# Half of a spatial chunk's transposing loads, asked ahead of the chunk before it

## The chip, the cores and the metric

The kernel runs on one core of a Trainium2 chip. The metric is the device time of one execution in microseconds, as the median of several runs. TensorE does the matmuls (PE in the profile), VectorE is DVE, ScalarE is ACT, GpSimd is POOL, and SyncE (SP) issues nearly all DMAs.

## The reference

Two branches read the same x (2048 rows of 1024) and are mixed by a gate per row. Branch A is a sliding, dilated attention with 32 heads; branch B is a gated MLP whose second half is mixed along the rows by a 2048 x 2048 matrix:

```python
g = sigmoid((x * gate_w).sum(-1, keepdims=True))
a = attention(x @ wqkv, window=8, dilation=2) @ wo
z = gelu(x @ w_in)                       # 2048 x 3584
z1, z2 = z[..., :1792], layernorm(z[..., 1792:])
mixed = w_sp @ z2 + b_sp[:, None]        # along the rows
b = (z1 * mixed) @ w_out
out = g * a + (1 - g) * b
```

## The kernel before

The program is one long stream on TensorE, and the work of the other engines is laid beside it by hand. A small planner, `beat`, keeps a virtual time: each group of matmuls calls `beat.run(columns)`, which moves the time on, and work registered by `beat.at(t, fn)` is put into the program at the first such point at or behind t. So `beat` fixes the order in which instructions stand in each engine's queue; it doesn't fix times on the chip. Each queue is worked off in order. A DMA on the SP queue that waits for something holds all DMAs behind it.

The order of the stages on TensorE: the columns of z2, then q, k and v of the attention (whose softmax runs on VectorE until late), then column tiles of z1, then the spatial product, then the output.

The part that matters here:

- Line 972: `for f in range(4, NF)` makes z1's column tiles f = 4 to 13, 32 matmuls each (line 983). The weights of four tiles at a time lie in one of two w1 buffers, `w1_slots[(f // 4) % 2]`: f = 8 to 11 use the first, f = 12 and 13 the second. A finished tile is stored to `z1_d` in DRAM (line 989). At f = 12, `load_z1c(0)` (line 515) is called, which brings 1.5 MB of z1 back for chunk 0.
- Lines 996 to 1023: `g_chunk(c)` is the spatial product for the output rows 512c to 512c + 511. Each of its 14 column tiles f is a chain of 16 matmuls (line 1010) of z2 against `wsp_slots[c]`. It is called for c = 0 and 1 (lines 1449 and 1450). The rows of chunks 2 and 3 are done by `seven_products` (line 1096), with fewer multiplications on sums and differences of blocks; its matmuls are those of line 1084.
- `wsp_slots[c]` holds 512 rows of w_sp, turned, so that the summed index lies on the partitions: 16 blocks i by 4 row groups aa by 128. `load_wsp(c, aa)` (line 512) fills one row group by a transposing DMA of 128 x 2048 values (512 KB). Chunk 1's buffer is the memory of the two w1 buffers: blocks i = 0 to 7 are the first, i = 8 to 15 the second.
- Lines 1426 to 1434 register, from t0 (the end of the z1 tiles) on: chunk 3's turned loads, the same rows of chunk 2 in natural order on ScalarE's queue (`natural`, line 1028), chunk 1's turned loads at t0 + 22, 26, 30 and 34, sums of absolute values on ScalarE (`sp_sums`) and a common scaling factor out of these, and chunk 2's loads at t0 + 50.
- `load_qk` (lines 413 to 415) and `load_v` (line 417) bring the next head group's q, k and v for VectorE, `store_o` (line 420) stores a pair of groups' result.
- The tile framework gives the DMAs eight completion counters in turn, and a DMA waits until the one before it on its counter has landed.

Of the kernel before, what the change touches and what calls it, by code (L numbers as in the profile page):

```python
# [58 lines left out]
def kernel(  # L59
# [24 lines left out]
    def reg(off, n):  # L84
        return arena[:, off:off + n]
# [11 lines left out]
    def warm_up(widths):  # L97
        pw = psum.tile([P, 512], F32, name="pw", tag="ps")
        for n in widths:
# [90 lines left out]
    wsp_slots = [reg(CD_OFF, 8192).rearrange("p (i a t) -> p i a t", i=16, a=4),  # L190
                 reg(EF_OFF, 8192).rearrange("p (i a t) -> p i a t", i=16, a=4),
                 reg(CD_OFF, 8192).rearrange("p (i a t) -> p i a t", i=16, a=4),
                 reg(X_OFF, 8192).rearrange("p (i a t) -> p i a t", i=16, a=4)]
# [42 lines left out]
    wsp_v = B_w_sp.rearrange("(a t) s -> a t s", t=P)  # L236
    wo_v = A_wo.rearrange("(g h d) n -> g h d n", g=NG, h=HG, d=DH)
    sync = nc.sync
# [40 lines left out]
    beat = Beat()  # L279
# [228 lines left out]
    def load_w1(ch):  # L508
        ncol = min(512, FH - 512 * ch)
        sync.dma_start(w1_slots[ch % 2][:, :, 0:ncol], win_v[:, :, 512 * ch:512 * ch + ncol])  # L510

    def load_wsp(c, aa):
        sync.dma_start_transpose(wsp_slots[c][:, :, aa, :], wsp_v[4 * c + aa])  # L513

    def load_z1c(c):
        sync.dma_start(z1c_slots[c][:, 0:12, :].rearrange("p f t -> p (f t)"), z1_d[c, :, 0:12 * 512])

# [445 lines left out]
    def seed(v):  # L963
        ps = psum.tile([P, 512], F32, name="ps", tag="ps")
        nc.scalar.copy(ps[:], v)
        seeded.append(ps)
# [5 lines left out]
    for f in range(4, NF):  # L972
        ch = f // 4
        w1 = w1_slots[ch % 2]
        if f == 8:
            load_w1(3)
        z1s = z1s_slots[(0, 1, 2, 3, 0, 1, 3, 2, 0, 3, 1, 2, 0, 1)[f]]
        for c in range(4):
            if 4 * f + c >= 4 * NF - AHEAD:
                seed(bsp_bc[:, 0:512])  # L980
            ps = psum.tile([P, 512], F32, name="ps", tag="ps")
            for kt in range(KT):
                nc.tensor.matmul(ps[:], w1[:, kt, (f % 4) * P:(f % 4 + 1) * P], xT[:, kt, 512 * c:512 * (c + 1)],  # L983
                                 start=(kt == 0), stop=(kt == KT - 1))
            keep = f > 11 and c < 2
            nc.scalar.activation(z1c_slots[c][:, f, :] if keep else z1s[:, c, :], ps[:], ACT.Gelu_apprx_tanh)
            beat.run(KT * 512)
        c0 = 2 if f > 11 else 0
        beat.at(beat.now + (3.0 if f < 11 else 0.0), lambda f=f, c0=c0, z1s=z1s: sync.dma_start(
            z1_d[c0:4, :, f * 512:(f + 1) * 512].rearrange("c p t -> p c t"), z1s[:, c0:4, :]))  # L990
        if f == 12:
            load_z1c(0)
# [35 lines left out]
    def natural(r):  # L1028
        nc.scalar.dma_start(nat_slots[r], wsp_v[8 + r])

    def sp_sums(r):
        for k in range(2):
            src = nat_slots[r][:, 1024 * k:1024 * (k + 1)] if r < 4 else wsp_slots[3][:, 8 * k:8 * k + 8, r - 4, :]
            dst = abs_wide if r < 4 else abs_wide.rearrange("p (i t) -> p i t", t=P)
            nc.scalar.activation(dst, src, ACT.Abs, accum_out=l1[:, r, k:k + 1])
# [8 lines left out]
    def scale_sp(c, aa):  # L1044
        v = wsp_slots[c][:, :, aa, :]
        nc.scalar.activation(v, v, ACT.Copy, scale=s_up[:].bitcast(F32))
# [377 lines left out]
    t0 = beat.now  # L1424
    s_steps = whole_power(s_up, omg[:, 8:16])
    for r in range(4):
        beat.at(t0 + 2.5 * r, lambda r=r: natural(r))
        beat.at(t0 + 0.5 + 2.5 * r, lambda r=r: load_wsp(3, r))
        beat.at(t0 + 22.0 + 4.0 * r, lambda r=r: load_wsp(1, r))
        beat.at(t0 + 12.0 + 3.2 * r, lambda r=r: sp_sums(r))  # L1430
        beat.at(t0 + 25.0 + 3.2 * r, lambda r=r: sp_sums(4 + r))
        beat.at(t0 + 50.0 + 3.0 * r, lambda r=r: load_wsp(2, r))
        beat.at(t0 + 53.0 + 3.5 * r, lambda r=r: scale_sp(3, r))
        beat.at(t0 + 66.0 + 3.0 * r, lambda r=r: scale_sp(2, r))
    beat.at(t0 + 39.0, lambda: load_z1c(1))
    beat.at(t0 + 38.0, sp_power)
    for k in range(2):
# [63 lines left out]
```

## Time and profile before

| | us |
|---|---|
| timed runs, median of 3 | 677.36 (677.0 to 677.49) |
| the profiled execution, its own time | 678.08 |
| span from its first to its last instruction | 676.0 |
| TensorE busy | 668.0 (99%) |
| VectorE busy | 564.1 (83%) |
| ScalarE busy | 443.7 (66%) |
| first matmul of chunk 0 of the spatial product | 355.97 |
| first matmul of chunk 1 | 405.48 |
| first matmul of the seven products | 453.83 |

The granted clock was 0.999. Times in the profile are from the span's start. "SPq" is a DMA issue on the SP queue, and its duration is the time for which the issue holds the queue. "Landing" is the time from the issue until the data is there. The matmuls follow each other by 0.216 us, though one of them is shown with 0.379 us, since they are pipelined. In the table by stretches the DMA share counts the packets' time, overlapping packets included, so that it can exceed 1.

### The profile page before, as it was taken

Reading aid. Unit: us, or ns where it says so; the run is one execution under the profiler, and the core shown is the slowest. Engines: PE = TensorE matmul, PEld = TensorE weight load, DVE = VectorE, ACT = ScalarE, POOL = GpSimd, SP = SyncE. Lnnn points to the kernel's source line nnn. Section 1 sums busy time; section 2 is a strip of 40 time slices with the busy share of each in tenths; the row PEclk is TensorE's granted clock in tenths of the full one; section 3 lists DMA queues with packets and bytes.
Section 4 is the critical chain, followed back from the end, with each engine's and each line's share of the span. In section 5 each row is a group of like instructions: output and inputs, shape, how many; then the busy total and the mean of one; then the engine's idle time right before and its main releaser. Section 6 shows DMA issues by size and latency. Waiting matters only on the chain.

```text
span 676.0 us, 8980 instructions
## 1 busy us (share of the span) xinstructions
PE 668.0 (99%) x3244; PEld 353.7 (52%) x3295; DVE 564.1 (83%) x690; ACT 443.7 (66%) x815; POOL 35.3 (5%) x68
## 2 busy tenths in 40 slices
PE   9999999999999999999999999999999999999997
PEld 4499666666654455644444444444444444444443
DVE  4669779999998999999999789989669888766653
ACT  4369888866888599986864996827977543323322
POOL 1000010000000001140110001000001001000000
PEclk9999999999999999999999999999999999999999
DMA  8994978355495893289849998202651514222210
GB/s 237 182 174 123 227 174 236 85 128 157 101 222 173 241 326 141 81 239 273 297 174 212 184 216 207 90 1 62 213 159 34 161 37 84 70 68 66 63 47 32
DMA packets 185305, 101.34 MB, mean 150 GB/s; under 512 B 143534, under 2 KB 172588, under 8 KB 185004
## 3 DMA queue, kind: packets, MB, share of 16 engines
q1 hardware_dynamic: 184396, 98.66, 56.2%
q10 hardware_dynamic: 576, 2.10, 1.5%
q8 instruction: 26, 0.43, 0.3%
q14 instruction: 19, 0.16, 0.1%
q0 software_dynamic: 288, 0.01, 0.0%
HBM read 56.95 MB, written 29.16 MB: 127 GB/s over the span
## 4 chain that ended last, share of the span: by engine, by line
PE 92%; SPq 6%; DMA 1%; issue 1%; another core or an unknown queue 0%; ACT 0%; DVE 0%
PE ps L673 16%; PE ps L310 14%; PE ps L1084 12%; PE ps L1216 12%; PE ps L983 10%; PE ps L696 7%; PE ps L1010 7%; PE ps L1305 6%; SPq L513 6%; PE ps L758 4%; PE ps L1295 1%; DMA arena<-in_B_w_sp_dram 1%; PE pw L100 0%; PE pt L326 0%
## 5 line engine op out<-in xcount | busy, mean ns | idle before, releaser
L673 PE MATMUL ps<-arena 128*128 128x512 bf16 (+1 forms) x637 | 114.9, 336 | 0.2
L310 PE MATMUL ps<-arena 128*128 128x512 bf16 (+1 forms) x501 | 98.0, 353 | 0.6
L1010 PE MATMUL ps<-arena 128*128 128x512 bf16 x439 | 96.5, 379 | 1.5 <-DMA arena<-in_B_w_sp_dram 1.0
L673 PEld LDWEIGHTS <-arena 128*128 128x128 bf16 x640 | 83.4, 144 | 27.7
L1216 PE MATMUL ps<-arena 128*128 128x512 f16 (+1 forms) x382 | 91.3, 379 | 0.4
L1084 PE MATMUL ps<-arena 128*128 128x512 f16 (+1 forms) x385 | 84.5, 379 | 0.4
L310 PEld LDWEIGHTS <-arena 128*128 128x128 bf16 x512 | 50.3, 98 | 47.4 <-issue 0.9
L1010 PEld LDWEIGHTS <-arena 128*128 128x128 bf16 x448 | 43.8, 98 | 54.1 <-issue 1.5
L404 DVE TENSOR_TENSOR arena<-arena,att_A 128x4096 bf16<-128x4096 bf16 (+1 forms) x23 | 71.6, 3120 | 0.0
L361 DVE TENSOR_TENSOR arena<-arena 128x8192 bf16<-128x8192 bf16 (+1 forms) x20 | 71.2, 3568 | 0.3
L983 PE MATMUL ps<-arena 128*128 128x512 bf16 x314 | 68.9, 379 | 0.3
L1084 PEld LDWEIGHTS <-arena 128*128 128x128 bf16 (+1 forms) x392 | 38.4, 98 | 46.3 <-issue 0.2
L1216 PEld LDWEIGHTS <-arena 128*128 128x128 f16 (+1 forms) x392 | 38.3, 98 | 46.3
L364 DVE TENSOR_TENSOR arena<-arena 128x4096 bf16<-128x4096 bf16 (+1 forms) x32 | 56.2, 1756 | 0.7
L696 PE MATMUL ps<-arena 128*128 128x512 f16 (+1 forms) x224 | 52.4, 379 | 0.0
L983 PEld LDWEIGHTS <-arena 128*128 128x128 bf16 x320 | 31.3, 98 | 37.5
L1305 PE MATMUL ps<-arena 128*128 128x512 f16 (+2 forms) x199 | 50.1, 375 | 0.2
L315 ACT ACTIVATE arena<-ps 128x512 bf16<-128x512 f32 x64 | 34.1, 539 | 22.8 <-PE ps L310 22.8
L1285 DVE SCALAR_TENSOR_TENSOR arena<-ps,g_s,arena 128x512 bf16<-128x512 f32 (+1 forms) x33 | 24.0, 734 | 29.2 <-ACT arena L1337 19.9
L682 ACT CAST arena<-ps 128x512 bf16<-128x512 f32 (+1 forms) x64 | 33.2, 550 | 12.7 <-PE ps L673 12.3
L696 PEld LDWEIGHTS <-arena 128*128 128x128 f16 (+1 forms) x224 | 32.3, 144 | 16.4 <-issue 0.3
L410 DVE TENSOR_TENSOR arena<-arena 128x4096 bf16<-128x4096 bf16 x16 | 36.6, 2287 | 0.2
(213 smaller groups left out, 865.0 us busy)
## 6 DMA issues: line engine op xcount, KB each, us to landing
arena<-v_d SPq DMA_DIRECT2D x8, 960.0 KB, 6.5
arena<-k_d SPq DMA_DIRECT2D x7, 960.0 KB, 6.0
arena<-in_A_wqkv_dram SPq DMA_DIRECT2D x24, 256.0 KB, 5.0
z_d<-arena SPq DMA_DIRECT2D x12, 512.0 KB, 4.3
arena<-in_B_w_in_dram SPq DMA_DIRECT2D x5, 1024.0 KB, 6.6
o_d<-arena SPq DMA_DIRECT2D x4, 1024.0 KB, 9.5
arena<-z_d SPq DMA_DIRECT2D x15, 256.0 KB, 3.4
out_dram<-arena SPq DMA_DIRECT2D x15, 256.0 KB, 2.2
```

Source lines behind the costliest of these rows:

```text
L310: nc.tensor.matmul(ps[:, 0:N], xT[:, kt, i * P:(i + 1) * P], w2[c][:, kt, 0:N], start=(kt == 0), stop=(kt == KT - 1))
L361: TT(prod.rearrange("p (w j c) -> p w j c", w=W, j=8, c=C)[:, w0:w1], in0, in1, ALU.mult)
L364: return lambda: TT(pv[:, :, 0:half], pv[:, :, 0:half], pv[:, :, half:2 * half], ALU.add)
L404: TT(prod.rearrange("p (w j d h) -> p w j d h", w=W, j=8, d=DH, h=HG)[:, w0:w1], in0, in1, ALU.mult)
L513: sync.dma_start_transpose(wsp_slots[c][:, :, aa, :], wsp_v[4 * c + aa])
L673: nc.tensor.matmul(ps[:, n0:n1].rearrange("p (t c) -> p t c", c=C), lhsT, wgt[:, pos0:pos1, kt, :], start=(kt == 0), stop=(kt == KT - 1))
L696: nc.tensor.matmul(dst[:].rearrange("p (t c) -> p t c", c=C), lhs(k), rhs[:, :, k, :], start=first and k == 0, stop=k == 3, skip_group_che ...
L983: nc.tensor.matmul(ps[:], w1[:, kt, (f % 4) * P:(f % 4 + 1) * P], xT[:, kt, 512 * c:512 * (c + 1)], start=(kt == 0), stop=(kt == KT - 1))
L1010: nc.tensor.matmul(ps[:], z2[:, f, i, :], wsp[:, i, :, :].rearrange("p a t -> p (a t)"), start=False, stop=(i == 15), skip_group_check=True)
L1084: nc.tensor.matmul(dst[:], lhs[:, k, :], rhs(k), start=False, stop=k == 7, skip_group_check=True)
L1216: nc.tensor.matmul(dst[:], lhs[:, j, :], rhs(j), start=first and j == 0, stop=j == 6, skip_group_check=not first)
L1305: nc.tensor.matmul(dst, lhs[:, k, :], rhs[:, k, :], start=first and k == 0, stop=k == 3, skip_group_check=not first)
```

## The change

Chunk 1's four turned loads are split by the blocks i, so that each becomes two loads of 128 x 1024 values (256 KB). The first halves (h = 0) fill the memory of the first w1 buffer. They are registered at the beginning of f = 12, at 5.0, 7.2, 9.4 and 11.6 us of the planner's time from there. The second halves (h = 1) stay where the whole loads were.

```diff
+    def load_wsp_half(c, aa, h):
+        sync.dma_start_transpose(wsp_slots[c][:, 8 * h:8 * h + 8, aa, :], wsp_v[4 * c + aa][:, 1024 * h:1024 * h + 1024])
...
     for f in range(4, NF):
...
+        if f == 12:
+            for aa in range(4):
+                beat.at(beat.now + 5.0 + 2.2 * aa, lambda aa=aa: load_wsp_half(1, aa, 0))
...
-        beat.at(t0 + 22.0 + 4.0 * r, lambda r=r: load_wsp(1, r))
+        beat.at(t0 + 22.0 + 4.0 * r, lambda r=r: load_wsp_half(1, r, 1))
```

In the built order the first early half stands on SP between the z1 store of f = 11 and `load_z1c(0)`. The other three stand between the z1 store of f = 12 and `load_qk` of the last head group, ahead of the store of f = 13 and of chunk 3's turned loads. The instructions of the other engines keep their order; some of their waits name other counters.

## The prediction

> **What bounds the kernel now.** I read the page first, then the chain of waits, then the timeline of TensorE and of the SP queue around line 513, and last the busy time by stretches. The page:
>
> ```profile
> PE 668.0 (99%) x3244; PEld 353.7 (52%) x3295; DVE 564.1 (83%) x690; ACT 443.7 (66%) x815; POOL 35.3 (5%) x68
> ...
> PE 92%; SPq 6%; DMA 1%; issue 1%; another core or an unknown queue 0%; ACT 0%; DVE 0%
> ```
>
> TensorE is busy for 668.0 of the span's 676.0 us. A change that touches no matmul can win only what is left, and most of that lies before the first matmul and after the last. The chain gives 6% to the SP queue; that is where to look.
>
> The chain of waits in order of time (start us, us, what), its part before chunk 1, and then TensorE's timeline from 330 to 460 us:
>
> ```profile
> 385.67 9.53 SPq L513
> 395.30 2.20 SPq L513
> 397.54 2.50 SPq L513
> 400.10 5.25 DMA arena<-in_B_w_sp_dram
> 405.48 9.01 PE ps L1010 x41
> ```
>
> ```profile
> 355.97 48.51 PE L1010 MATMUL ps<-arena 128*128 128x512 bf16 x219
> 405.48 48.51 PE L1010 MATMUL ps<-arena 128*128 128x512 bf16 x220 [1.00 <-DMA arena<-in_B_w_sp_dram]
> 453.83 6.42 PE L1084 MATMUL ps<-arena 128*128 128x512 bf16 x28
> ```
>
> Chunk 0 of the spatial product starts at 355.97, chunk 1 at 405.48, the products after it at 453.83. Chunk 1 therefore takes 453.83 - 405.48 = 48.35 us without a stall. Chunk 0 is as long, so TensorE was ready for chunk 1 at 355.97 + 48.35 = 404.32. It waited 405.48 - 404.32 = **1.16 us** for the last of chunk 1's four turned loads, issued at 400.10 and landed at 405.35. (The row says 1.00, because the modelled end of a matmul overlaps the next by 0.16.) No other wait of TensorE after the start comes near it: the groups of matmuls have 0.0 to 0.6 us of idle time each, the group of line 1010 has 1.5.
>
> Why the last load is late is in the SP queue's timeline, and in the busy time by stretches (PE, PEld, DVE, ACT, POOL busy, clock, DMA share, GB/s):
>
> ```profile
> 349.88 0.36 SPq L989 DMA_DIRECT2D z_d<-arena  x1
> 354.99 0.33 SPq L414 DMA_DIRECT2D arena<-q_d  x1
> 355.37 0.43 SPq L415 DMA_DIRECT2D arena<-k_d  x1
> 356.79 0.37 SPq L989 DMA_DIRECT2D z_d<-arena  x1
> 357.26 27.00 SPq L513 DMA_TRANSPOSE arena<-in_B_w_sp_dram  x4
> 384.36 0.52 SPq L418 DMA_DIRECT2D arena<-v_d  x1
> 384.98 0.63 SPq L422 DMA_DIRECT2D o_d<-arena  x1
> 385.67 17.63 SPq L513 DMA_TRANSPOSE arena<-in_B_w_sp_dram  x4
> ```
>
> ```profile
> 344.00:350.00 6.00, 5.95 (x29) 2.72 (x28) 5.90 (x4) 3.02 (x6) 0.00 (x0) 1.00 0.62 206
> 350.00:357.00 7.00, 7.00 (x34) 3.16 (x33) 6.86 (x6) 4.44 (x9) 0.38 (x4) 1.00 0.57 186
> 357.00:372.00 15.00, 14.89 (x69) 6.82 (x70) 13.48 (x13) 5.57 (x11) 0.00 (x0) 1.00 1.12 228
> 372.00:385.00 13.00, 12.95 (x61) 5.88 (x61) 8.73 (x12) 12.91 (x27) 0.00 (x0) 1.00 1.13 164
> 385.00:405.00 20.00, 19.37 (x89) 8.62 (x88) 16.71 (x22) 19.81 (x42) 0.02 (x1) 1.00 1.12 230
> ```
>
> From 357 to 405 the DMA engines are full (share 1.12 to 1.13). SP is held by the four loads for chunk 3 (27.00 us), then v and o, then chunk 1's four (17.63 us). From 344 to 357 the share is only about 0.6 and SP stands idle for most of the time.
>
> **The change, part by part.** *The early halves.* Four loads of 256 KB are put ahead. In the built order the first stands behind the z1 store of f = 11 (issued 343.63) and ahead of load_z1c(0) (346.74); the other three stand behind the store of f = 12 (349.88 + 0.36 = 350.24) and ahead of load_qk (354.99), the store of f = 13 and chunk 3's loads. Their target was the w1 buffer of f = 8 to 11, and f = 12 and 13 follow with 2 x 32 matmuls of 0.216 us, 13.8 us before 355.97: it is free at 342.1, so the halves wait for no matmul.
>
> The duration: 256 KB turned loads are in the trace at other places. Line 484 has a median of 1.28 us on SP (least 1.23, most 3.28), line 547 1.31; the 512 KB loads of line 513 have a least of 2.20 and a median of 3.49. Two halves cost 2.56 against 2.20, so the split costs about 0.36 us of SP per load, 1.4 us in all, none of it TensorE's. The Trainium skill ("DMA: Bandwidth & Descriptors", section "Rules for kernel authors") speaks against such a split: it asks for large transfers and for small ones to be put together. The trace agrees in direction (205 GB/s at 1.28 us, 238 at 2.20), and if half of the loss fell on the late halves they would land 0.7 us later, which the sum below has room for.
>
> The first half has SP free for 2.5 us (it waited at 516 for a store to land), so it costs nothing. The other three are bounded from both sides. On a quiet queue they take 3 x 1.28 = 3.84, end at 354.1, before load_qk's own time, and delay nothing. Under load, at half of the loaded rows (5.11 and 10.94), they take 7.7 to 16.4 us and end at 357.9 to 366.7. I take a value between, by the data ahead of them: load_z1c(0) needs 6.7 us from its issue (median of that size), so it is in at 353.4, and 3 x 1.28 behind it ends at 357.2. Then load_qk is issued 2.2 us late. It has cover: its q and k are first read by the product at 383.40 on VectorE. Behind it the f = 13 store goes at 358.1 and chunk 3's first load at about 358.6 in place of 357.26, **1.3 us late**. Chunk 3's loads feed sums on ScalarE from 387.75 to 400.5, and ScalarE ran these without waiting.
>
> The loads share eight completion counters in turn, and four more move them by four places: the ScalarE queue's natural rows now wait for early halves to land. The second (issued 360.05) waits for the last early half: 357.2 less 1.28 plus a landing of 4.2 (line 547) is 360.1, no wait to speak of. Behind it on ScalarE are chunk 0's copies and seeds, and these are five tiles (5 x 3.46 = 17 us) ahead of TensorE.
>
> *The late halves.* From v's issue (384.36) to the last landing (405.35) are 20.99 us, in which about 4 MB move (1 of v, 1 of o, 2 of chunk 1). One MB less at that rate is 5.2 us less. Bounds: half of the three undisturbed issues, (2.20 + 2.50 + 3.20) / 2 = 4.0; half of all four (17.43 / 2) = 8.7. I take 5.2, since the DMA engines are full there. The last half lands at 405.35 + 1.3 - 5.2 = **401.4**, 2.9 us before TensorE is ready at 404.32. The stall of 1.16 us goes.
>
> A row and a rule on the 1.3 us: the loads at 362.41 and 370.83 took 8.38 and 10.94 us while the natural rows moved on ScalarE's queue, the next one 2.44. The Trainium skill ("DMA: Bandwidth & Descriptors", section "Queues, rings and completion order") says that an engine with work on several queues takes a packet of each in turn. The trace agrees: 256-byte packets of the turned loads against 4096-byte ones. By that rule a later start of chunk 3's loads is partly absorbed, as they wait for the natural rows anyway: the last half would land between 400.1 and 401.4, and the slide told of below would be less likely than its rows alone make it.
>
> *What is late next.* TensorE begins chunk 1 1.16 us earlier, and the rest must keep up. VectorE is dense from 402 to 449, but waits for TensorE's results at 449.6 to 451.2 (1.59) and before 452.30 (0.69), so it moves up by more than 1.16. The nearest later one is the sums for the second of the seven products: they end at 467.92, and are needed by its third product at 453.83 + 12.10 + 3.46 = 469.39, 1.47 us of room. Chunk 2's loads wait for chunk 0's last matmul, at 404.5 in both, and z1c(1), behind the late halves, moves up. I find nothing that takes the 1.16 us back.
>
> **Sum.** Span 676.0 - 1.16 = 674.8; the profiled execution 678.08 - 1.16 = 676.92. The median of the timed runs is 677.36, 0.72 below the profiled one; the change comes off it as it stands: **676.20**, which is -0.17%. About 0.2% (1.35 us) is what a measurement of this kernel can tell from no change, so the likeliest outcome is just inside "same".
>
> **Rivals.** *The timed runs stall by another length.* The wait hangs on DMA times, and the runs spread from 677.0 to 677.49. If the 0.72 us of the profiled run are stall, the timed gain is 0.44: 676.9. If the timed runs wait longer by as much as their spread (0.49), it is 1.65: 675.7, faster by 0.24%. For the first speaks that the profiled run is the slowest; for the second, nothing but the spread.
>
> *The gain is taken back behind chunk 1.* If VectorE does not follow, the sums at 467.92 leave 0.3 us at best; a VectorE half a microsecond behind that returns 0.2: 676.4.
>
> *Slower: the three early halves hold SP, and all behind it slides.* Place: SP from 350.24. If they do not end before the natural rows start (359.63), they crawl as chunk 3's loads did, at 5.5 us each. At the worst they end at 366.7, 11.7 us behind load_qk's time; with the smaller saving of 4.0 the last late half lands at 405.35 + 11.7 - 4.0 = 413.1, a stall of 8.7, 7.6 more than now: 684.9. With the saving of 5.2 it decides from a slide of 4.2 us on (2.9 + 1.3), where a stall is back; from 5.4 on it is slower than before and from 6.7 on measurably. Against it: load_z1c(0) is the only large transfer then, and DMA share is 0.57.
>
> *The change does not do what it says.* Excluded by the built order: the eight half loads stand where described, and chunk 1's first matmul waits for four loads, its ninth for the other four.
>
> **Chances.** Stall gone, within 0.2%: 0.48. Stall gone and more than 1.35 us in the timed runs: 0.30 (only 0.19 us more than the profiled stall is needed). Partly returned or smaller: 0.06, also within. The slide: 0.16, nearly all of it slower. The range goes from the long stall, 675.7, to no gain at all, 677.4; the slide beyond it is left out, with a little below.
>
> **What would show it.** Chunk 1 follows chunk 0 by 48.35 us, with no wait for in_B_w_sp; the chain has no SP queue at 360 to 400; SP shows half loads near 344 and 350 to 357, load_qk at 355 to 357.2, chunk 3's first load near 358.6, and four late halves that end before 400. DMA share at 344 to 357 rises towards 1. I am wrong if SP's early halves last beyond 359.6, if chunk 1 still waits, or if another wait of about 1 us shows behind 453.

## The result, and the profile after

The change made the kernel slower, by a little under 1%. Six runs of the changed kernel have a median of 683.93 us (680.55 to 687.38), six of the kernel before on the same chip 677.53 (677.0 to 677.7). The ratio is 1.0095, with a 95% interval of 1.0078 to 1.0112. The profiled execution took 687.38 us, its span 685.5, which is 9.5 us more than the profiled 676.0 of before. It is the slowest of its six, so the profile shows the loss large.

The page of the changed kernel, its busy line, its chain, and the row of the spatial product (line 1010 before, 1016 now):

```profile
PE 670.5 (98%) x3244; PEld 353.9 (52%) x3295; DVE 563.9 (82%) x690; ACT 444.0 (65%) x815; POOL 35.3 (5%) x68
...
PE 29%; DVE 2%; issue 0%; ACT 0%; DVEq 0%
...
L1016 PE MATMUL ps<-arena 128*128 128x512 bf16 x439 | 98.4, 383 | 5.3 <-ACT ps L968 4.6
```

The wait for `in_B_w_sp` is gone from the row. In its place TensorE waits 4.6 us for line 968. That is a seed: ScalarE copies the starting values of a tile into PSUM, and TensorE adds on top. The chain, followed back from the last instruction, breaks off on VectorE at about 462 us and no longer leads to SP: the engine that was late, ScalarE, is one that the prediction had taken for covered. TensorE's timeline from 357 to 560 us (start, us, what, and in brackets the idle time before it and its releaser):

```profile
357.30 34.87 PE L1016 MATMUL ps<-arena 128*128 128x512 bf16 x157
394.94 1.56 PE L1016 MATMUL ps<-arena 128*128 128x512 bf16 x5 [2.77 <-ACT ps L968]
396.72 17.33 PE L1016 MATMUL ps<-arena 128*128 128x512 bf16 x73 [0.22 <-issue]
415.90 45.05 PE L1016 MATMUL ps<-arena 128*128 128x512 bf16 x204 [1.84 <-ACT ps L968]
460.79 3.62 PE L1090 MATMUL ps<-arena 128*128 128x512 bf16 x16
465.98 12.26 PE L1090 MATMUL ps<-arena 128*128 128x512 f16 x55 [1.57 <-DVE arena L1067]
479.17 69.33 PE L1090 MATMUL ps<-arena 128*128 128x512 f16 x314 [0.93 <-DVE arena L1078]
548.34 10.74 PE L1222 MATMUL ps<-arena 128*128 128x512 bf16 x48
```

The 9.5 us are made up as follows. Chunk 0 begins 1.33 us later (357.30 against 355.97). This comes from the start of the kernel, long before the changed lines: at 36.50 us against 35.15 TensorE is that far behind already, mostly by 1.0 us in which line 310 waited for loads of w_in. Chunks 0 and 1 take 460.79 - 357.30 = 103.49 us, where two chunks without a stall take 2 x 48.35 = 96.70. So they lose 6.79, and lost 1.16 before: +5.63. The seven products take 548.34 - 460.79 = 87.55 against 84.70 before: +2.85. What follows them is 0.31 shorter. 1.33 + 5.63 + 2.85 - 0.31 = 9.5.

Why the seeds were late is in ScalarE's timeline, in the groups of the natural rows (line 1029 before, 1035 now), and on SP. First ScalarE from 366 to 388 us:

```profile
366.51 0.59 ACT L968 CAST ps<-arena 128x512 f32<-128x512 bf16 x1 [1.51 <-DMA arena<-k_d]
...
371.17 0.59 ACT L968 CAST ps<-arena 128x512 f32<-128x512 bf16 x1 [2.72 <-DMA z_d<-arena]
371.69 0.58 ACT L1024 CAST arena<-ps 128x512 bf16<-128x512 f32 x1
385.08 1.06 ACT L1041 ACTIVATE arena<-arena 128x1024 bf16<-128x1024 bf16 x1 [12.81 <-DMA arena<-in_B_w_sp_dram]
...
387.93 0.58 ACT L968 CAST ps<-arena 128x512 f32<-128x512 bf16 x1
```

ScalarE works its queue in order. At 372.27 it came to the sum over the first natural row and stood there for 12.81 us, with chunk 0's next seeds behind it in its queue. The landing times of the four natural rows, of the kernel before and then of the changed one:

```profile
L1029 ACTq DMA_DIRECT2D arena<-in_B_w_sp_dram x4: 335/366/448, 359.6 to 366.5; - x4
...
DMA to landing us min/median/max: 8.4/14.4/17.0
```

```profile
L1035 ACTq DMA_DIRECT2D arena<-in_B_w_sp_dram x4: 334/357/699, 361.0 to 370.8; - x4
...
DMA to landing us min/median/max: 20.1/23.5/25.1
```

The first two were issued 1.3 us later, as the whole stage was. The third and fourth came 3.1 and 4.3 us later (366.13 and 370.79): before these issues ScalarE waited 1.51 us for k and 2.72 for a store of z1 to land. ScalarE uses neither, so these are waits for completion counters. But all four needed 20 to 25 us instead of 8 to 17, the first one too. The SP queue at the same time:

```profile
351.63 5.43 SPq L516 DMA_TRANSPOSE arena<-in_B_w_sp_dram  x3
357.11 0.58 SPq L414 DMA_DIRECT2D arena<-q_d  x1
...
358.74 35.95 SPq L513 DMA_TRANSPOSE arena<-in_B_w_sp_dram  x4
394.79 0.53 SPq L418 DMA_DIRECT2D arena<-v_d  x1
395.41 0.63 SPq L422 DMA_DIRECT2D o_d<-arena  x1
396.10 11.63 SPq L516 DMA_TRANSPOSE arena<-in_B_w_sp_dram  x4
```

The early halves stand and end where the prediction put them (how far this is luck is said below). But chunk 3's four loads (line 513) took 35.95 us instead of 27.00. So two streams became slower together, for the same bytes: the turned loads on SP and the natural rows on ScalarE's queue. The busy time by stretches (PE, PEld, DVE, ACT, POOL busy, clock, DMA share, GB/s) shows it best, the two streams' time before and then after:

```profile
359.60:384.30 24.70, 24.59 (x114) 11.19 (x115) 19.22 (x23) 17.52 (x35) 0.00 (x0) 1.00 1.13 184
```

```profile
361.00:394.80 33.80, 31.05 (x142) 13.96 (x143) 15.89 (x16) 13.63 (x26) 0.00 (x0) 1.00 1.14 149
```

The DMA engines are as busy as before (1.14 against 1.13) and move 149 GB/s instead of 184. They are not short of work; they do it more slowly. In what follows this state is called the crawl. The packets themselves show it, counted from the trace by their size. In the changed kernel from 366 to 390 us a 256-byte packet of the turned loads took 18 ns in the median, but 115 in the mean: 39% of them took over 150 ns, and these make up 90% of the time. For the 4096-byte packets of the natural rows the mean is 315 ns. In the run below that lets the two streams move one behind the other ("held until the natural rows are in") the means are 20 and 166 ns. The kernel before stands between them (65 and 253 ns from 366 to 382 us), so it has a milder form of the same slowness.

### The profile page after: what moved, and what is told of

It reads as the page before. It is cut to its first block, busy times and chain, and to the rows that moved or that the text cites. A ratio compares the mean times of both kernels' runs of the same rounds, so it can differ in the third digit from the quotient of the medians.

```text
span 685.5 us, 8986 instructions
## 1 busy us (share of the span) xinstructions
PE 670.5 (98%) x3244; PEld 353.9 (52%) x3295; DVE 563.9 (82%) x690; ACT 444.0 (65%) x815; POOL 35.3 (5%) x68
## 5 line engine op out<-in xcount | busy, mean ns | idle before, releaser
L1016 PE MATMUL ps<-arena 128*128 128x512 bf16 x439 | 98.4, 383 | 5.3 <-ACT ps L968 4.6
L989 PE MATMUL ps<-arena 128*128 128x512 bf16 x314 | 68.9, 379 | 0.3
L315 ACT ACTIVATE arena<-ps 128x512 bf16<-128x512 f32 x64 | 34.1, 539 | 24.1 <-PE ps L310 24.1
```

Source lines behind the costliest of these rows:

```text
L1016: nc.tensor.matmul(ps[:], z2[:, f, i, :], wsp[:, i, :, :].rearrange("p a t -> p (a t)"), start=False, stop=(i == 15), skip_group_check=True)
```

## The experiments

Theories at the outset: the natural rows wait behind other completion counters, since four more DMAs shift them; more bytes ahead of load_qk and chunk 3's loads; something in the turned loads themselves; or the two streams disturbing each other when they start in a certain order. Each ratio is to the kernel before on the same chip, whose medians were 677.48 to 677.65.

**One, two and three of the early halves.** The edit, with n = 1, 2 or 3; the other row groups stay whole and late:

```diff
-            for aa in range(4):
+            for aa in range(n):
...
-        beat.at(t0 + 22.0 + 4.0 * r, lambda r=r: load_wsp_half(1, r, 1))
+        beat.at(t0 + 22.0 + 4.0 * r, lambda r=r: load_wsp_half(1, r, 1) if r < n else load_wsp(1, r))
```

> Only the first row group's half load goes early (ahead of load_z1c(0)); row group 0's other half and the other three whole loads stay in the late place. Contention (the early loads ahead of load_qk push q, k and the f = 13 store into the natural rows and chunk 3's turned loads, which then crawl together): nothing new is ahead of load_qk, so the natural rows land as before (8 to 17 us after their issue), ScalarE does not wait for them, the last turned load of chunk 1 lands about 1.3 us earlier and the stall of 1.16 us goes: 676.2 to 676.6. Counters (more DMAs move the completion counters, so that the natural rows on ScalarE's queue wait for other loads): one place moved, part of the loss is there, 678 to 681.

> Two of the four half loads go early (one ahead of load_z1c(0), one ahead of load_qk). Mixing (the natural rows on ScalarE's queue and the 256-byte packets of turned loads on SP's crawl together, and the loss depends on how much of chunk 3's first load gets through before the natural rows begin): the second half fits into SP's idle time before load_qk's own time, so chunk 3's first load starts as before: natural rows land within 17 us, 676.3 to 677.3. If every turned load ahead of load_qk costs by itself: about a third of the change's loss, 678 to 680.

> Three of the four half loads go early, two of them ahead of load_qk. Mixing: load_qk is issued up to half a microsecond late, its data are in shortly before the natural rows begin: near the edge, 676.5 to 680, with more spread than with two. If every turned load ahead of load_qk costs by itself: two thirds of the loss, 680 to 682.

Measured: 677.59 us, 1.000 [0.9991, 1.001] for one; 677.32, 1.000 [0.9991, 1.001] for two; 676.86, 0.9993 [0.9984, 1.0002] for three. The natural rows' median landing was 14.4, 10.3 and 15.7 us, load_qk went at 354.69, 355.12 and 354.99, and the wait for chunk 1's loads was gone from all three profiles. So splitting is harmless and moving is harmless, but the gain expected of the first of them (676.2 to 676.6) isn't there either. The loss comes with the fourth half, and with it load_qk is pushed for the first time, to 357.11.

**Four tiny loads, and four plain loads, added to the kernel before at the places of the early halves.** The first brings only the four DMAs (8 KB each), the second the four times 256 KB without turning:

```diff
+        if f == 12:
+            for aa in range(4):
+                beat.at(beat.now + 5.0 + 2.2 * aa, lambda aa=aa: sync.dma_start(
+                    reg(EF_OFF + 1024 * aa, 32), wsp_v[4 + aa][:, 0:32]))      # plain4: 1024 in place of 32
```

> The kernel before with four loads of 8 KB (128 x 32 values) at the places of the four early halves, into memory that the whole late loads overwrite. The counters move by four as in the change, but no bytes to speak of move. Contention: 677.4, natural rows land within 17 us. Counters: the loss of the change is there, 681 to 685, and ScalarE waits for natural rows for over 5 us.

> The kernel before with four plain (not turned) loads of 256 KB at the places of the four early halves, into memory that the whole late loads overwrite, so nothing is saved later. Contention by bytes: load_qk's data come later by about the time of these bytes, natural rows land over 18 us after their issue, TensorE stalls: 680 to 686. If only turned loads do the harm: 677.4 to 678. Counters: 681 to 685.

Measured: 677.25 us, 1.0003 [0.9992, 1.0013] for the tiny loads, natural rows 13.8 us; 677.00, 0.9991 [0.9982, 1.0001] for the plain ones, natural rows 11.4 us. Neither crawls. The shifted counters are not the cause by themselves, nor are the bytes. In the changed kernel the counters did hold two rows back, as shown above; but the first row, which no counter held, was late all the same, and the kernel with the hold on k, further down, has the wait for the store of z1 too (2.7 us) and no loss.

**The same bytes, plain, in pieces of 256 bytes.** The turned loads move 256-byte packets. Here plain loads do:

```diff
+                beat.at(beat.now + 5.0 + 2.2 * aa, lambda aa=aa: sync.dma_start(
+                    wsp_slots[1][:, 0:8, aa, :], wsp_v[4 + aa][:, 0:1024].rearrange("t (i q) -> t i q", q=P)))
```

> As the run with four plain early loads, but each written in pieces of 256 bytes (128 values for each block i), so that the early loads have the packet size of the turned ones without turning; the whole late loads overwrite them. If it is small packets ahead of load_qk that push its data back: load_qk is late by 0.5 us or more, natural rows land after 18 us, 680 to 685. If it is the turning: 677.0 to 677.6, as with large packets.

Measured: 679.23 us, 1.0031 [1.0011, 1.005], with ten runs from 676.95 to 687.49. So the early loads need not be turned for a loss; small packets at these places bring one, in part of the runs. That it is the same loss isn't shown: the profiled run (678.90) has natural rows of 16.2 us and a wait of 1.7 us for chunk 1's loads; its large losses were not profiled.

**The natural rows on SP's queue.** The changed kernel, with one word changed, so that the natural rows and chunk 3's loads alternate on one queue; later the same word in the kernel before:

```diff
-        nc.scalar.dma_start(nat_slots[r], wsp_v[8 + r])
+        nc.sync.dma_start(nat_slots[r], wsp_v[8 + r])
```

> The changed kernel with the four natural rows of chunk 2 issued on the SP queue in place of ScalarE's, at the same planner times, so that they and the turned loads go through one queue one after the other. Contention between the two queues: the crawl goes, natural rows land within 10 us of their issue, ScalarE waits for them for less than 3 us, no stall at chunk 1: 676.0 to 676.8. Contention by bytes alone, whatever the queue: 680 to 685. Counters: 680 to 685.

> The kernel before (whole loads, no early halves), with the natural rows issued on SP's queue. Mixing: natural rows land within 10 us, chunk 3's loads end at about 380, chunk 1's whole loads land by 400, the stall of before goes without any early half: 676.3 to 676.9, as the changed kernel with the same edit. If the early halves are needed for the gain: 677.3 to 677.6.

Measured, with the change: 676.73 us (676.11 to 676.86), 0.9984 [0.9975, 0.9994]. This is faster than both kernels, by 0.76 us against the kernel before. Without the change: 677.34, 0.9996 [0.9988, 1.0005], though 676.3 to 676.9 was expected and its profile shows no stall. The busy time by stretches and TensorE's timeline of the first:

```profile
357.70:379.70 22.00, 22.00 (x104) 9.94 (x103) 17.89 (x17) 12.45 (x24) 0.00 (x0) 1.00 1.10 257
```

```profile
356.38 96.86 PE L1016 MATMUL ps<-arena 128*128 128x512 bf16 x448
453.07 84.86 PE L1090 MATMUL ps<-arena 128*128 128x512 bf16 x392
```

The same rows now move at 257 GB/s, the natural rows land after 4.5 us (median), and TensorE runs both chunks and the seven products in one piece each. The early halves are all there, and load_qk goes at 356.15. The loss needs the two queues at once.

**Chunk 3's loads held until the natural rows are in.** The changed kernel, with an 8 KB store of the last natural row into a new DRAM tile n_d on SP ahead of chunk 3's loads. SP has to wait for that row:

```diff
-        beat.at(t0 + 0.5 + 2.5 * r, lambda r=r: load_wsp(3, r))
+        beat.at(t0 + 10.0 + 0.5 * r, lambda r=r: load_wsp(3, r))
...
+    beat.at(t0 + 9.0, lambda: sync.dma_start(n_d[:], nat_slots[3][:, 0:32]))
```

> The changed kernel with a store of 8 KB of the last natural row, to memory that nothing reads, on SP ahead of chunk 3's four turned loads, so that SP holds these back until the natural rows have landed. Mixing: the two never run together; natural rows land within 9 us of their issue, chunk 3's loads then take about 2.5 us each and end at 385 at the latest although they start 12 us later, ScalarE does not wait for natural rows, no stall at chunk 1: 676.0 to 677.0. If bytes or the early halves do the harm: chunk 3's loads start later and all is worse than in the change, 686 to 692.

Measured: 676.86 us, 0.9993 [0.9984, 1.0002], natural rows 6.1 us. Its SP queue:

```profile
370.22 0.32 SPq L1442 DMA_DIRECT2D n_d<-arena  x1
370.63 9.53 SPq L514 DMA_TRANSPOSE arena<-in_B_w_sp_dram  x4
380.26 0.53 SPq L419 DMA_DIRECT2D arena<-v_d  x1
```

Chunk 3's loads start 12 us later than in the changed kernel (370.63 against 358.74) and end 14.5 us earlier. Alone they take 9.53 us, not 35.95.

**Chunk 3's loads late, in the kernel before.** Is it that these loads start late against the natural rows? An 8 KB store of k ahead of them holds them until k has landed:

```diff
+    beat.at(t0 + 0.2, lambda: sync.dma_start(n_d[:], k_t[:, 14 * C:14 * C + 32]))
```

> The kernel before, with no early loads at all, and a store of 8 KB of k (just loaded) on SP ahead of chunk 3's four turned loads, to memory that nothing reads: SP holds these until k has landed, at about 362 in place of 357.3, behind the start of the natural rows (359.6). Mixing: as in the change, chunk 3's first two loads take over 25 us together (13.5 before), natural rows land 18 us or more after their issue, ScalarE waits for one of them for over 5 us; 681 to 688. If it needs the early turned halves: natural rows land within 17 us and ScalarE does not wait; everything behind is only some 4 us later, so that chunk 1 waits about 5 us: 681 to 682.

Measured: 677.58 us, 0.9998 [0.9987, 1.001]. The loads start at 363.08, 5.8 us later than before, take 20.45 us, and the natural rows land after 9.6. Both expectations had a loss; there is none, so being late does no harm by itself, and this form of the theory fell. Counted from the trace's packets, 804 KB of the natural rows had started before the first packet of chunk 3's loads, at 365.02.

**The fourth early half behind load_qk.** In the changed kernel, so that load_qk isn't pushed:

```diff
-                beat.at(beat.now + 5.0 + 2.2 * aa, lambda aa=aa: load_wsp_half(1, aa, 0))
+                beat.at(beat.now + (5.0, 7.2, 9.4, 14.1)[aa], lambda aa=aa: load_wsp_half(1, aa, 0))
```

> The changed kernel with the fourth early half moved behind load_qk and the store of f = 13, directly ahead of chunk 3's turned loads; the bytes ahead of these stay, but load_qk is no longer pushed. If the push of q and k decides: as with three early halves, 676.6 to 677.0, natural rows land within 17 us. If what decides is when chunk 3's first load gets through ahead of the natural rows: it is as late as in the change, natural rows land after 18 us, 680 to 687.

Measured: 680.26 us, 1.0038 [1.0016, 1.0059], ten runs from 676.54 to 682.95: four below 677.7, six above 679.5. The profile is of the fastest run and shows no crawl (natural rows 11.4 us). The push of load_qk isn't needed for a loss. The loss is there or not there from run to run.

**The changed kernel again, with the same hold on k, and with the natural sums later.** Three together on one chip. The hold is the edit of the kernel before, above. The other lets the four sums over natural rows stand 12 us further back among ScalarE's work, behind more seeds:

```diff
-        beat.at(t0 + 12.0 + 3.2 * r, lambda r=r: sp_sums(r))
+        beat.at(t0 + 24.0 + 3.2 * r, lambda r=r: sp_sums(r))
```

> The changed kernel once more, on the chip and beside the runs of the next two. If the loss is the crawl of the two queues, it comes in varying amounts: 678 to 688 over the runs, median about 683; natural rows landing over 18 us after their issue in the profile if that run is over 681.

> The changed kernel with the store of 8 KB of k on SP ahead of chunk 3's loads, which holds these until k has landed (about 365). Simultaneous start (the two streams crawl when both begin with all of their bytes ahead of them, and one that has a lead of half a megabyte or more gets through): the natural rows get the lead, land within 14 us, chunk 3's loads end by 386, no wait of ScalarE: 676.4 to 677.6 although these loads start 6 us later. Lateness (any later start of chunk 3's loads costs): worse than the change, 685 to 690.

> The changed kernel with the four sums over natural rows on ScalarE registered 12 us later, behind more of chunk 0's copies and seeds. The DMA side is as in the change. If ScalarE's wait for natural rows is what carries the delay to TensorE: the natural rows still land after over 18 us in slow runs, but ScalarE waits under 5 us and chunk 0 has no stall; what is left is the late chunk 3 loads and late halves, a stall of 2 to 4 us at chunk 1: median 679 to 681. If the delay comes over SP's queue alone: 682 to 685 as in the change.

Measured: the changed kernel 682.03 us, 1.0074 [1.005, 1.0097], and its second profile (685.13) crawls again: natural rows 22.1 us, chunk 3's loads 33.95, ScalarE's longest wait for a natural row 11.5; with the hold 676.60, 0.9989 [0.998, 0.9999]; with later sums 678.70, 1.0012 [0.9995, 1.0029]. SP of the second:

```profile
365.39 0.32 SPq L1442 DMA_DIRECT2D n_d<-arena  x1
365.81 17.66 SPq L514 DMA_TRANSPOSE arena<-in_B_w_sp_dram  x4
383.56 0.53 SPq L419 DMA_DIRECT2D arena<-v_d  x1
```

Chunk 3's loads start 7 us later than in the changed kernel and end 11 us earlier, and the natural rows land after 9.2 us. One small store that waits undoes the whole loss, with the early halves and load_qk (357.77) as late as in the changed kernel or later. TensorE's timeline of the third:

```profile
357.03 50.24 PE L1016 MATMUL ps<-arena 128*128 128x512 bf16 x232
408.36 46.78 PE L1016 MATMUL ps<-arena 128*128 128x512 bf16 x216 [1.09 <-DMA arena<-in_B_w_sp_dram]
454.98 15.70 PE L1090 MATMUL ps<-arena 128*128 128x512 bf16 x72
470.93 69.33 PE L1090 MATMUL ps<-arena 128*128 128x512 f16 x320 [0.25 <-DVE arena L1078]
```

Here the crawl is in full (natural rows 21.7 us, chunk 3's loads 33.90), but ScalarE waits for natural rows only 2.2 us in all, no seed is late, and what is left is 1.09 us for the late halves and 0.25 behind. The median drops by 682.03 - 678.70 = 3.3 us of the 4.4 lost on that chip. So most of the loss goes through ScalarE's queue, and the rest, at least in the profiled run (679.14), through SP. The stall before chunk 1 is shorter than the 2 to 4 us expected.

## Why the prediction was wrong

**What held.** The stall before chunk 1 was read rightly. In all kernels with early halves and no crawl, TensorE runs the two chunks as one block. The early halves ended at 357.06 (forecast 357.2), load_qk went at 357.11 (357.2) and chunk 3's first load at 358.74 (358.6). That these agree so well is luck: against before load_qk is 2.1 us late and chunk 3's first load 1.5, but 1.33 of each is the later start of the whole stage in this run, which the forecast did not have. And the three halves behind the store of f = 12 did not wait for load_z1c(0) and then take 3.84 us; they started at once and took 5.43. The late halves were sized about rightly: chunk 1's group took 11.63 us of SP in place of 17.63, 6.0 less (forecast 5.2), the last three 1.30 to 1.32 each, close to the 1.28 that were used. The split costs nothing that TensorE sees.

**The step that failed** is the one that ends "Chunk 3's loads feed sums on ScalarE from 387.75 to 400.5, and ScalarE ran these without waiting", with the paragraph on counters that follows. It moved chunk 3's loads by 1.3 us and left their length at 27.00; they took 35.95. And it priced the issue of one natural row ("no wait to speak of"), not the two counter waits of 1.51 and 2.72 us behind it, and not at all the landing of the rows. That was a term put at nothing, and it is the one that decided: ScalarE waited 12.81 us for the first row. The profile of before had the number to see that this cover was thin: the first natural row was issued at 359.63 and first read by ScalarE at 370.46, so 10.8 us later, and the four rows took 8.4 to 17.0 us to land. At least 8.4 of the 10.8 were needed: at most 2.4 us of room, against the "17 us" of seeds that the prediction set between ScalarE and TensorE. With a first landing 24.1 us after its issue (360.96 to 385.08) ScalarE stood for those 12.81, and with the sums and the other work that stood ahead of the next seeds the cover was used up.

**The rule on packets.** The prediction drew from the Trainium skill ("DMA: Bandwidth & Descriptors", section "Queues, rings and completion order") that a DMA engine takes the packets of its queues in turn, and took from it that a later start of chunk 3's loads is partly absorbed. Its words "the trace agrees" say too much, since the rows that it names give the sizes of the packets and not their turns. Read that way, the natural rows, with 4096-byte packets against 256, should win beside turned loads, and the order of the starts should change who waits rather than the total. The runs speak against this use of it: natural rows landed in 4.5 us without a second queue and in 23.5 beside it, and the total went from 257 to 149 GB/s. The Trainium skill says on the same page ("DMA: Bandwidth & Descriptors", section "Rules for kernel authors") that spreading DMAs over several issuing engines for bandwidth doesn't help. Here it cost some: 149 and 184 GB/s on two queues against 257 on one.

**The rivals.** The slower rival came near in time (684.9; 683.93 measured) and in place (SP behind 350). Its mechanism was another, so the nearness in time is luck. It had the early halves hold SP up to 366.7; they ended at 357.06. It had chunk 1's late halves stall TensorE; these did slide, by about 9 us beyond the stage's own later start (v's issue 394.79 against 384.36), but TensorE, held up by the seeds, did not wait for them. In the run with later sums, where v went 2.25 us earlier, they cost 1.09. In the changed kernel the loss went through the seeds. The rival "gain taken back behind chunk 1" has a part too, and so has the last of the prediction's signs of being wrong: two stalls of 1.57 and 0.93 us in the seven products, which the profiles without a crawl don't have. There VectorE was behind by more than that rival's half microsecond (line 1067 began 11.3 us later than in the kernel before, the products 7.0); it had itself stood 13.28 us for a copy of ScalarE.

**The size of the gain.** A stall of 1.16 us in the profile was taken as 1.16 in the timed runs. Kernels whose profile shows no stall measured between 0.1 us slower and 1.05 us faster: one and two early halves, and the natural rows on SP and the hold on k without the change, 0.1 slower to 0.2 faster; the plain loads 0.5; three halves, the hold until the rows are in, 0.6; the hold on k with the change 1.05, natural rows on SP with the change 0.76. Only the last two have intervals that exclude no change. So the 1.16 is an upper end that most timed runs don't reach, and the chance for "faster" was too high even without the crawl.

**What the runs show of the cause, and what stays open.** Shown: the loss of the changed kernel needs chunk 3's turned loads and the natural rows in flight on two queues (on one queue it is gone), and it is gone too when one stream is held until the other has a lead or is through. Counters, bytes, the push of load_qk and late loads are excluded as the cause by themselves. That the crawl comes when both streams start at nearly the same moment is the reading that fits. Counted from the packets, in the three profiles that crawl (the changed kernel twice, and with later sums) the turned loads led the natural rows by only 0.5 to 0.8 us and 75 to 90 KB. In every other profile on two queues one stream led by 1.4 us or more: with one to three halves the turned loads had 376 to 498 KB started first, with the hold on k the natural rows 804 (without the change) and 976 KB. It is argued from the packets' times, not shown by a run that sets this moment alone, and how much lead is enough is not known. Open are why single packets take so long in the crawl, and why the same kernel has runs without it (the fastest of the kernel with its fourth half behind load_qk took 676.54, the slowest 682.95); a losing run of that kernel was not profiled, so that its loss is the crawl isn't shown.

## What to carry to other kernels

Before filling the idle stretch of a DMA queue, look at what two queues start together behind it, and read the landing times of that other queue's loads against the moment of their first reader: room of 2 us is no cover when loads take 8 to 17. If two large loads must run in the same stretch, try them on one queue, or let one wait for the other by a small store that reads what the other brings; here both took the loss away. A sum or copy that waits for a DMA on an in-order engine which also feeds TensorE belongs as far back in that engine's queue as its own reader allows.

## What the runs showed of the hardware that was not expected

Two streams of about 2 MB each, 256-byte packets from SP's queue and 4096-byte packets from ScalarE's, moved, with all else in those stretches, between 149 GB/s (35.95 us for the turned one) and 257 GB/s (on one queue); one behind the other, the turned one took 9.53 us. The DMA share was above 1 in both (1.14 and 1.10), so a full share doesn't tell a good stretch from a bad one; GB/s beside it does.

TensorE paid for the 2.77 us stall twice. The granted clock behind it, by stretches of the changed kernel:

```profile
392.00:394.90 2.90, 0.17 (x1) 0.00 (x0) 0.00 (x0) 2.87 (x8) 0.00 (x0) 1.00 1.05 234
394.90:397.00 2.10, 1.84 (x6) 0.84 (x7) 1.46 (x5) 2.10 (x5) 0.00 (x0) 0.70 1.37 217
397.00:399.00 2.00, 2.00 (x6) 0.75 (x5) 1.97 (x3) 1.97 (x5) 0.00 (x0) 0.50 0.84 242
399.00:401.00 2.00, 2.00 (x11) 0.85 (x10) 2.00 (x1) 1.97 (x4) 0.00 (x0) 0.97 1.00 337
```

The columns are those of the stretches above. The clock is 0.70, 0.50 and 0.97 in the three stretches after the stall: 0.30 x 2.1 + 0.50 x 2.0 + 0.03 x 2.0 = 1.7 us lost. With the waits of 2.77, 0.22 and 1.84 this makes 6.5 of the 6.79 us that the two chunks lost. The Trainium skill ("TensorE: Matmul & The Clock Gate", section "What's actually happening") has the clock fall to half after an idle window of about 3.4 us and return after a busy one, in windows that run freely. The way back agrees: the trace has the clock at half from 395.73 us on for 3.41 us. The fall doesn't fit a wholly idle window, since TensorE stood for only 2.77 us. The second stall of this run (1.84 us) and the longest of the second profile of the changed kernel (3.12 us) were not followed by a lower clock, so the length of a stall alone doesn't tell what it costs.
